# One kernel, two ways of holding P: some thirds of the attention weights kept as one float32 copy

## The chip, the cores and the metric

The kernel runs on one core of a Trainium2 chip. The core has a matrix engine (TensorE; PE in the profile, with PEld for its weight loads), a vector engine (VectorE, DVE), an activation engine (ScalarE, ACT), a general engine (GpSimd, POOL) and a queue that starts transfers (SyncE, SP). Each works through its own instructions in order, and they wait for each other by semaphores. On-chip memory has 128 partitions; TensorE writes its results to a small second memory, PSUM. The metric is the time of one execution on the device, in microseconds (us).

## The reference

Pooled attention over 4 batches and 8 heads, then two feed-forward layers. In float32:

```
q, k, v : (4, 8, 1152, 64)
q_pool = q.reshape(B, H, S // 2, 2, D).mean(axis=3)          # 576 queries
scores = matmul(q_pool, k^T) / sqrt(D)                       # 576 x 1152
attn   = exp(scores - max);  attn = attn / (sum + 1e-9)
x      = matmul(attn, v)                                     # -> (2304, 512)
h  = x @ w_in ;  g  = maximum(0.01 * h, h) ;         y   = g  @ w_out    # 512 -> 2048 -> 512
h2 = y @ w_in2;  g2 = where(h2 > 0, h2, exp(min(h2,0)) - 1); out = g2 @ w_out2
```

The weights of both layers arrive as 64-bit floats and are turned into float32 on the chip.

## The kernel before

**How float32 products are made.** TensorE is used with the type `float32r`, in which one pass goes over float32 numbers at reduced precision. To keep precision, each operand is split into two parts, hi (the value rounded to that type) and lo (the value less hi). `psplit` (line 256) makes them: ACT or DVE copies to hi, DVE or POOL subtracts. A product then takes two or three matmuls.

**Attention.** Heads are worked in pairs, 16 pairs in all (4 per batch), by `attn_pair` (line 550). A pair has nine tiles of 128 query rows: four for each head and one that holds the last 64 rows of both. For a tile, `scores` (line 434) computes three thirds of 384 keys in PSUM (line 452), DVE takes the maxima (lines 457, 459), ACT takes the exponentials with their sums into the tile `p` (line 463). `transpose_p` (line 469) then turns each third round: three transposes on TensorE (line 475), and out of PSUM twice, first by ACT as hi (line 261 of `psplit`) and then, once that is done, by DVE as lo (line 267). They land in a tile `pt`, one for each third, of which four buffers exist (`PTB`). `pv` (line 485) multiplies: for each third, three chunks of 128 keys, with hi and lo, so six matmuls (line 496) of 256 or 320 query columns. Its stationary operand `vn` holds v's hi part in 64 columns and its lo part in the other 64, so the two halves of the result are added afterwards (lines 507 and 509). A pair has four such calls, over 256, 320, 320 and 256 columns. `normalise` (line 511) divides by the sums.

**Feed-forward.** `mlp` runs each layer of each batch in 16 steps `f`: up (line 629) and down (line 667) matmuls of 288 columns, with the activation between (lines 640 to 650) and the sums of the output (line 680). `load_w` brings the weights, and `convert` (line 273; DVE at lines 293, 296 and 305, ACT at 299 and 301, POOL at 303) turns 64-bit into 32-bit. This happens once per layer; later batches load the kept result.

**What sets the order.** All work is entered into `Program` as pieces with an engine, a cost in nanoseconds, a rank and dependencies. Before the program is built a list schedule with these costs fixes the order of the pieces on every engine: whenever an engine is free, the ready piece with the lowest rank goes next. A pair takes nine ranks; the feed-forward of batch b begins when that batch's four pairs are done and shares the time of the next batch's pairs. For the last batch both layers come after the last pair.

The costs of the pieces concerned are written at the calls: three transposes 3 x 107 ns, P V for a third `6 * max(107, 0.42 * n)`.

Of the kernel before, what the change touches and what calls it, by code (L numbers as in the profile page):

```python
# [9 lines left out]
F32 = mybir.dt.float32  # L10
F32R = mybir.dt.float32r
U32 = mybir.dt.uint32
ACTF = mybir.ActivationFunctionType
# [141 lines left out]
def kernel(  # L155
# [20 lines left out]
    V, A, G, PE = nc.vector, nc.scalar, nc.gpsimd, nc.tensor  # L176
# [5 lines left out]
    NP = H // 2  # L182
# [8 lines left out]
    PTB = 4  # L191
# [17 lines left out]
    WLEAD = 1.5  # L209
    SBUFS = 3  # L210
    RAWB = 3
    EARLY = {'s': 'sss', 't': 'tthh'}
    T1B = 3
    HBUFS = 2
# [7 lines left out]
    ORDER = (0, 1, 2)  # L222
# [3 lines left out]
    PVLAG = 0.5  # L226
# [8 lines left out]
    def f32(ap):  # L235
        return ap.bitcast(F32)
# [4 lines left out]
    prog = Program()  # L241

    def sb(tag, shape, dt=F32, bufs=1):
        return prog.buf(tag, bufs, lambda: sp.tile(shape, dt, tag=tag, name=tag, bufs=bufs))

    def bank(tag, shape, dt=F32, bufs=1):
        return prog.buf(tag, bufs, lambda: ps.tile(shape, dt, tag=tag, name=tag, bufs=bufs))

    def act(n, accum=False, sbuf=False):
        return 50 + 0.833 * n + (190 if accum else 0) + (43 if sbuf else 0)  # L250

    def dve(n, fast=False):
        return 66 + (0.52 if fast else 1.05) * n
# [4 lines left out]
    def psplit(rank, h, l, hi, lo, src, n, w, r, w_l=None, fast=True, psum=False):  # L258

        if h == "ACT":  # L260
            prog.add("ACT", act(n, sbuf=not psum), rank, lambda: A.activation(out=hi(), in_=src(), func=ACTF.Copy), w=[w], r=r)  # L261
        else:
            prog.add("DVE", dve(n, fast), rank, lambda: V.tensor_copy(out=hi(), in_=src()), w=[w], r=r)
        eng = V if l == "DVE" else G
        prog.add(
            l, dve(n) if l == "DVE" else pool(n), rank,
            lambda: eng.tensor_tensor(out=lo(), in0=src(), in1=f32(hi()), op=ALU.subtract),  # L267
            w=[w_l or (w[0], "l")], r=[w] + r)
# [69 lines left out]
    for j in range(2):  # L338
        t = sp.tile([128, 2, 128], F32R, name=f"rem{j}")
# [6 lines left out]
    def load(rank, key, tag, shape, pieces, bufs):  # L346
        t = sb(tag, shape, F32, bufs)
        for i, (to, src) in enumerate(pieces):
            prog.add("SP", 60, rank, lambda to=to, src=src: nc.sync.dma_start(out=to(t), in_=src), w=[(t, i)])
        raw[key] = t  # L350

    def load_kq(rank, b, hp, j):
        h = 2 * hp + j
        load(rank, (b, hp, j, "k"), "raw", [128, KC, D],
             [(lambda t: t.ap, k[b, h].rearrange("(p c) d -> p c d", c=KC))], RAWB)
        load(rank, (b, hp, j, "q"), "raw", [128, KC, D],
             [(lambda t: t[:, 0:2 * QT, :], q[b, h, 0:256 * QT].rearrange("(p r) d -> p r d", r=2 * QT))], RAWB)

    def load_v(rank, b, hp, j):
        load(rank, (b, hp, j, "v"), "raw", [128, KC, D],  # L360
             [(lambda t: t.ap, v[b, 2 * hp + j].rearrange("(p c) d -> p c d", c=KC))], RAWB)

    def load_rem(rank, b, hp):
        load(rank, (b, hp, "x"), "qrem", [128, 2, D],
             [(lambda t, j=j: t[64 * j:64 * j + 64],
               q[b, 2 * hp + j, 256 * QT:S].rearrange("(p r) d -> p r d", r=2)) for j in range(2)], 2)
# [37 lines left out]
    def prep_q(rank, b, hp, j):  # L404
        qn = q_split(rank, raw[b, hp, j, "q"], QT, "q")
        qT = sb("qT", [128, 2, QT, 128], F32R, KTB)
        for a in range(2):
            t = tr_r(rank, (qn, a), lambda i, a=a: qn[:, a, i, :], QT)
            prog.add("ACT", act(512), rank, lambda t=t, a=a: A.activation(
                out=qT[:, a], in_=f32(t.ap), func=ACTF.Copy), w=[qT], r=[t])  # L410
        prep[b, hp, j, "q"] = qT
# [20 lines left out]
    def pbank(use, dt=F32, shape=(128, 4, 128)):  # L432
        tags = (EARLY if first_window[0] else {}).get(use, use)
        n = turns[use] = turns.get(use, -1) + 1
        tag = tags[n % len(tags)]
        return bank(tag, list(shape), dt, BANKS[tag])
# [29 lines left out]
                w=[(p, c), (total, (idx, c))], r=[banks[c], (m, 3)])  # L466
        return p

    def transpose_p(rank, p, dests):
        for c in ORDER:  # L470
            t = pbank("t")

            def tr(t=t, c=c):
                for i in range(3):
                    PE.transpose(  # L475
                        out=t[:, i, :], in_=p[:, (3 * c + i) * 128:(3 * c + i + 1) * 128],
                        identity=ident)

            prog.add("PE", 3 * 107, rank, tr, w=[t], r=[(p, c)])
            for pt, c0, s0, n in dests:  # L480
                hi = lambda a=0, pt=pt, c=c, c0=c0, n=n: pt[c][:, a, :, c0:c0 + n]
                psplit(rank, "ACT", "DVE", hi, lambda hi=hi: hi(1), lambda t=t, s0=s0, n=n: t[:, 0:3, s0:s0 + n],
                       3 * n, (pt[c], ("h", c0)), [t], (pt[c], ("l", c0)), fast=False, psum=True)

    def new_pt(n):
        pt = {c: sb("pt", [128, 2, 3, n], F32R, PTB) for c in ORDER}
        return pt

    def pv(rank, b, hp, j, pt, col0, n):
        o = pbank("o", F32, (128, 512))  # L490
        vn = prep[b, hp, j, "v"]

        def mm(th):
            for c in range(3 * th, 3 * th + 3):
                for a in range(2):
                    PE.matmul(  # L496
                        out=o[:, 0:n], lhsT=vn[:, c, :], rhs=pt[th][:, a, c % 3, :],
                        start=(c == 3 * ORDER[0] and a == 0), stop=(c == 3 * ORDER[2] + 2 and a == 1))

        for th in ORDER:  # L500
            prog.add("PE", 6 * max(107, 0.42 * n), rank + PVLAG, lambda th=th: mm(th), w=[o], r=[vn, pt[th]])
        if (b, hp) not in xu:
            xu[b, hp] = sb("xu", [128, NQ], F32, XFB)
        x = xu[b, hp]
        hi, lo = slice(64 * j, 64 * j + 64), slice(64 - 64 * j, 128 - 64 * j)
        tm = sb("tm", [128, 5 * 64])
        prog.add("ACT", act(n), rank + PVLAG, lambda: A.activation(
            out=tm[hi, 0:n], in_=o[lo, 0:n], func=ACTF.Copy), w=[tm], r=[o])
        prog.add("DVE", dve(n), rank + PVLAG, lambda: V.tensor_tensor(
            out=x[hi, col0:col0 + n], in0=o[hi, 0:n], in1=tm[hi, 0:n], op=ALU.add),  # L510
            w=[(x, (j, col0))], r=[o, tm])
# [37 lines left out]

    def attn_pair(at, b, hp, nxt):  # L550
        pts = {}
        n1 = 128 + 128 + RQ
        sums[b, hp] = sb("sum", [128, n9, 3], F32, 2)

        def tile_(at, j, t, g, c0, new=None):
            qT = prep[b, hp, j, "q"]
            p = scores(at, b, hp, [(j, qT, lambda a: qT[:, a, t, :])], 2 * t + j)
            if new:
                pts[j, g] = new_pt(new)
            transpose_p(at, p, [(pts[j, g], c0, 0, 128)])  # L560

        if nxt:
            load_kq(at, *nxt, 0)
            load_rem(at, *nxt)
            load_v(at + 2, *nxt, 0)
            load_kq(at + 3, *nxt, 1)
            load_v(at + 4, *nxt, 1)
        tile_(at, 0, 0, 0, 0, 256)
        prep_k(at + PREP, b, hp, 1)
        prep_q(at + PREP, b, hp, 1)  # L570
        tile_(at + 1, 0, 1, 0, 128)
        prep_rem(at + PREP, b, hp)
        pv(at + 1, b, hp, 0, pts[0, 0], 0, 256)
        prep_v(at + 1, b, hp, 1)
        tile_(at + 2, 0, 2, 1, 0, n1)
        tile_(at + 3, 0, 3, 1, 128)
        p = scores(at + 4, b, hp, [
            (j, rem_t[j], lambda a, j=j: rem_t[j][:, a, :]) for j in range(2)], 2 * QT)
        pts[1, 1] = new_pt(n1)
        transpose_p(at + 4, p, [(pts[0, 1], 256, 0, 64), (pts[1, 1], 256, 64, 64)])  # L580
        pv(at + 4, b, hp, 0, pts[0, 1], 256, n1)
        tile_(at + 5, 1, 2, 1, 0)
        tile_(at + 6, 1, 3, 1, 128)
        if nxt:
            prep_k(at + 5, *nxt, 0)
            prep_q(at + 5.5, *nxt, 0)
            prep_v(at + 6, *nxt, 0)
        pv(at + 6, b, hp, 1, pts[1, 1], 256, n1)
        tile_(at + 7, 1, 0, 0, 0, 256)
        tile_(at + 8, 1, 1, 0, 128)  # L590
        pv(at + 8, b, hp, 1, pts[1, 0], 0, 256)
        normalise(at + 8 + PVLAG + 0.2, b, hp)


# [136 lines left out]
    for b, layer, at, wide in PLAN:  # L731
        tags = [(u, size[u]) for u in ("h" * HBUFS + ("t" * TB + "s" * SBUFS if wide else ""))]
        w = ((moe_w_in, moe_w_out), (moe2_w_in, moe2_w_out))[layer]
# [35 lines left out]
```

## Time and profile before

| | |
|---|---|
| median of 3 runs | 1545.18 us (1543.68 to 1550.88) |
| the profiled execution, as a run | 1545.34 us |
| its span in the trace | 1543.5 us |
| PE busy | 1414.5 us (92%) |
| PEld busy | 1365.2 us (88%) |
| DVE busy | 1011.4 us (66%) |
| ACT busy | 1065.9 us (69%) |
| POOL busy | 830.3 us (54%) |
| granted TensorE clock | 0.99 of 2.4 GHz on average |

Shares are averages over stages that differ: in the first 16 of 40 equal slices DVE is at 8 or 9 tenths in all but the very first; after them it falls to 6 and less while PE goes to 9 in nearly all. The end of a matmul in the trace is modelled, and matmuls overlap, so what one costs is read from the distance between starts (a run of n of them, divided), and "PE busy" holds some overlap of one group's tail with the wait behind it.

### The profile page before, as it was taken

The page shows a single profiled execution, that of the slowest core. Times are in us where ns is not written, and L with a number is a line of the kernel's source. Part 1 is how long each engine was busy: PE and PEld are TensorE (multiplying, and loading weights), DVE is VectorE, ACT ScalarE, POOL GpSimd, SP SyncE. Part 2 cuts the span into 40 slices and gives each one's busy share as a digit, 9 for nine tenths or more (in the row PEclk, how much of TensorE's full clock was granted, in tenths as well). Part 3 has the DMA queues.
Part 4 walks back from the last instruction along what each step waited for, and adds up shares of the span by engine and source line. Part 5 has one row for each costly group of instructions (what it writes and reads, how often), then busy time and mean ns, then how long its engine had stood idle before and what let it go on. Part 6 is the DMA issues. An engine that isn't in the chain of part 4 may idle for free.

```text
span 1543.5 us, 28953 instructions
## 1 busy us (share of the span) xinstructions
PE 1414.5 (92%) x10288; PEld 1365.2 (88%) x10288; DVE 1011.4 (66%) x2273; ACT 1065.9 (69%) x2901; POOL 830.3 (54%) x840
## 2 busy tenths in 40 slices
PE   5878889888888898999999999999999999899997
PEld 4777788888878887999999999899999998899897
DVE  6999889899998998556565556645665554124222
ACT  6989878776678787676668776676667763443553
POOL 5443255765766667254555556254554445466662
PEclk9999999999999999999999999999999999999999
DMA  4332123343334443222222222222221121322221
GB/s 138 99 115 87 40 75 123 121 130 125 126 118 144 130 143 120 74 71 73 67 69 86 79 78 63 74 76 66 71 67 59 55 56 56 93 76 82 69 82 39
DMA packets 82642, 135.59 MB, mean 88 GB/s; under 512 B 8512, under 2 KB 26944, under 8 KB 82496
## 3 DMA queue, kind: packets, MB, share of 16 engines
q1 hardware_dynamic: 82496, 133.73, 28.0%
q8 instruction: 81, 1.33, 0.4%
q14 instruction: 65, 0.53, 0.1%
HBM read 112.20 MB, written 21.50 MB: 87 GB/s over the span
## 4 chain that ended last, share of the span: by engine, by line
PE 64%; DVE 21%; ACT 6%; issue 3%; DMA 3%; POOL 2%; SPq 0%; ACTq 0%; POOLq 0%; DVEq 0%
PE h L667 17%; PE h L629 16%; PE s L452 8%; PE o L496 7%; PE t L475 5%; DVE m L457 3%; PE s L629 3%; DVE ct L293 3%; DVE wr L305 3%; DVE ct L296 3%; DVE pt L267 2%; PE s L667 2%; PE t L373 2%; PE t L629 2%; PE t L667 2%
## 5 line engine op out<-in xcount | busy, mean ns | idle before, releaser
L667 PE MATMUL h<-g,wo 128*128 128x288 f32 x2544 | 437.1, 302 | 17.5 <-DVE t L650 7.9
L629 PE MATMUL h<-xs,wi 128*128 128x288 f32 x2520 | 429.2, 305 | 22.9 <-DVE t L650 14.2
L629 PEld LDWEIGHTS h<-xs,wi 128*128 128x128 f32 x2520 | 362.5, 190 | 32.5 <-DVE t L650 20.0
L667 PEld LDWEIGHTS h<-g,wo 128*128 128x128 f32 x2544 | 367.1, 188 | 23.8 <-DVE t L650 9.6
L457 DVE TENSOR_REDUCE m<-s 128x1 f32<-128x384 f32 x432 | 232.2, 550 | 74.4 <-PE s L452 71.6
L261 ACT ACTIVATE pt<-t 128x384 fp32r<-128x384 f32 (+1 forms) x416 | 184.0, 457 | 115.2 <-PE t L475 108.3
L463 ACT ACTIVATE p<-s,m 128x384 f32<-128x384 f32 x432 | 249.5, 588 | 18.3 <-DVE m L459 18.0
L267 DVE TENSOR_TENSOR pt<-t,pt 128x384 fp32r<-128x384 f32 (+1 forms) x416 | 206.8, 509 | 73.3 <-ACT pt L261 71.7
L267 POOL TENSOR_TENSOR g<-t,g 128x288 fp32r<-128x288 f32 x256 | 211.1, 831 | 79.9 <-ACT g L261 75.5
L267 POOL TENSOR_TENSOR wo<-wr,wo 128x512 fp32r<-128x512 f32 x128 | 166.4, 1304 | 137.5 <-ACT wo L261 134.3
L452 PE MATMUL s<-kT,qT 128*128 128x384 f32 x768 | 197.0, 354 | 25.4 <-ACT p L463 24.5
L267 POOL TENSOR_TENSOR wi<-wr,wi 128x512 fp32r<-128x512 f32 x128 | 167.6, 1309 | 91.9 <-ACT wi L261 79.3
L496 PE MATMUL o<-pt,vn 128*128 128x256 f32 (+1 forms) x1152 | 192.5, 303 | 5.5 <-DVE pt L267 3.6
L475 PE MATMUL t<-ident,p 128*128 128x128 f32 x1116 | 181.6, 277 | 12.4 <-DVE pt L267 11.7
L496 PEld LDWEIGHTS o<-pt,vn 128*128 128x128 f32 x1152 | 165.5, 190 | 10.6 <-DVE pt L267 10.2
L475 PEld LDWEIGHTS t<-ident,p 128*128 128x128 f32 x1116 | 139.4, 142 | 22.1 <-DVE pt L267 12.3
L452 PEld LDWEIGHTS s<-kT,qT 128*128 128x128 f32 x768 | 125.5, 192 | 32.2 <-ACT p L463 31.0
L303 POOL TENSOR_TENSOR ct<-ct,cr 128x256 uint32<-128x256 uint32 x128 | 98.8, 774 | 96.7 <-DVE ct L296 29.8
L261 ACT ACTIVATE g<-t 128x288 fp32r<-128x288 f32 x256 | 112.2, 445 | 49.0 <-DVE t L650 28.4
L267 POOL TENSOR_TENSOR vn<-raw,vn 128x576 fp32r<-128x576 f32 x32 | 46.4, 1449 | 174.4 <-ACT vn L261 174.4
L261 ACT ACTIVATE wo<-wr 128x512 fp32r<-128x512 f32 x128 | 80.6, 630 | 78.9 <-PE h L667 47.5
L680 DVE TENSOR_TENSOR acc<-h,acc 128x288 f32<-128x288 f32 x158 | 71.1, 452 | 67.2 <-PE h L667 66.1
(106 smaller groups left out, 2080.0 us busy)
## 6 DMA issues: line engine op xcount, KB each, us to landing
wr<-w SPq DMA_DIRECT2D x192, 256.0 KB, 2.6
cr<-in_moe_w_in_dram SPq DMA_DIRECT2D x64, 256.0 KB, 2.7
cr<-in_moe_w_out_dram SPq DMA_DIRECT2D x64, 256.0 KB, 2.7
w<-wr SPq DMA_DIRECT2D x64, 256.0 KB, 2.4
raw<-in_k_dram SPq DMA_DIRECT2D x32, 288.0 KB, 3.0
raw<-in_v_dram SPq DMA_DIRECT2D x32, 288.0 KB, 3.1
raw<-in_q_dram SPq DMA_DIRECT2D x32, 256.0 KB, 2.9
out_dram<-cr SPq DMA_DIRECT2D x16, 256.0 KB, 2.1
```

The lines of the kernel that those rows point to most:

```text
L261: prog.add("ACT", act(n, sbuf=not psum), rank, lambda: A.activation(out=hi(), in_=src(), func=ACTF.Copy), w=[w], r=r)
L267: lambda: eng.tensor_tensor(out=lo(), in0=src(), in1=f32(hi()), op=ALU.subtract),
L293: prog.add("DVE", dve(CW, True), rank, lambda r=r, t=t: V.tensor_scalar(out=t.ap, in0=r[:, :, 1], scalar1=3, scalar2=0x3FFFFFF8, op0=ALU.l ...
L303: prog.add("POOL", pool(CW), rank, lambda t=t, r=r: G.tensor_tensor(out=t.ap, in0=t.ap, in1=r[:, :, 0], op=ALU.add), w=[t], r=[t, (r, 0)])
L452: PE.matmul(out=st[:, 0:384], lhsT=qa(a), rhs=kT[:, 384 * c:384 * c + 384], start=(i == 0), stop=(i == len(seq) - 1))
L457: prog.add("DVE", dve(384), rank - LR, lambda st=st, c=c: V.tensor_reduce(out=m[:, c:c + 1], in_=st[:, 0:384], axis=AX.X, op=ALU.max), w=[ ...
L463: prog.add("ACT", act(384, True), rank - LE, lambda c=c: A.activation(out=p[:, 384 * c:384 * c + 384], in_=banks[c][:, 0:384], func=ACTF.E ...
L475: PE.transpose(out=t[:, i, :], in_=p[:, (3 * c + i) * 128:(3 * c + i + 1) * 128], identity=ident)
L496: PE.matmul(out=o[:, 0:n], lhsT=vn[:, c, :], rhs=pt[th][:, a, c % 3, :], start=(c == 3 * ORDER[0] and a == 0), stop=(c == 3 * ORDER[2] + 2 ...
L629: PE.matmul(out=h[:, 0:HB], lhsT=wi[:, a, c, :], rhs=xs[c][:, e, cols], start=(c == 0 and a == 0 and e == 0), stop=(c == DC - 1 and a == 1))
L667: PE.matmul(out=y[:, 0:HB], lhsT=w[f][1][:, a, d * 128:(d + 1) * 128], rhs=g[f][:, e, cols], start=(f % FC == 0 and a == 0 and e == 0), st ...
L680: prog.add("DVE", dve(HB), rank - HURRY, lambda y=y, a_=a_, cols=cols: V.tensor_tensor(out=a_[:, cols], in0=y[:, 0:HB], in1=a_[:, cols], o ...
```

## The change

In the first batch (pairs 0 to 3) two of the three key thirds of P, and in pairs 4 to 9 one, are no longer split. The transposed third is copied out of PSUM once, as float32, by DVE or by ACT (`WHOLE` says which), and `pv` multiplies it by v's two stacked parts read as float32, in three matmuls in place of six. The list schedule gets a new cost for these pieces, 5.25 ns per column for a third as float32, and 2.76 for one in two parts in place of `6 * max(107, 0.42 * n)`. The other thirds, and pairs 10 to 15, are computed as before.

```diff
+    WHOLE = ({0: "DVE", 1: "ACT"}, {0: "ACT"})
+    WPAIRS = 10
...
-    def transpose_p(rank, p, dests):
+    def transpose_p(rank, p, dests, whole):
         for c in ORDER:
             t = pbank("t")
+            how = whole.get(c)
...
             prog.add("PE", 3 * 107, rank, tr, w=[t], r=[(p, c)])
             for pt, c0, s0, n in dests:
+                if how:
+                    o, i_ = (lambda pt=pt, c=c, c0=c0, n=n: pt[c][:, :, c0:c0 + n],
+                             lambda t=t, s0=s0, n=n: t[:, 0:3, s0:s0 + n])
+                    if how == "ACT":
+                        prog.add("ACT", act(3 * n), rank, lambda o=o, i_=i_: A.activation(
+                            out=o(), in_=i_(), func=ACTF.Copy), w=[(pt[c], ("h", c0))], r=[t])
+                    else:
+                        prog.add("DVE", dve(3 * n), rank, lambda o=o, i_=i_: V.tensor_copy(
+                            out=o(), in_=i_()), w=[(pt[c], ("h", c0))], r=[t])
+                    continue
                 hi = lambda a=0, pt=pt, c=c, c0=c0, n=n: pt[c][:, a, :, c0:c0 + n]
                 psplit(rank, "ACT", "DVE", hi, lambda hi=hi: hi(1), lambda t=t, s0=s0, n=n: t[:, 0:3, s0:s0 + n],
                        3 * n, (pt[c], ("h", c0)), [t], (pt[c], ("l", c0)), fast=False, psum=True)
 
-    def new_pt(n):
-        pt = {c: sb("pt", [128, 2, 3, n], F32R, PTB) for c in ORDER}
+    def new_pt(n, whole):
+        pt = {c: sb("pt", [128, 3, n], F32, PTB) if c in whole else sb("pt", [128, 2, 3, n], F32R, PTB) for c in ORDER}
         return pt
...
             for c in range(3 * th, 3 * th + 3):
-                for a in range(2):
+                for a in range(1 if th in whole else 2):
                     PE.matmul(
-                        out=o[:, 0:n], lhsT=vn[:, c, :], rhs=pt[th][:, a, c % 3, :],
+                        out=o[:, 0:n], lhsT=f32(vn[:, c, :]) if th in whole else vn[:, c, :],
+                        rhs=pt[th][:, c % 3, :] if th in whole else pt[th][:, a, c % 3, :],
                         start=(c == 3 * ORDER[0] and a == 0), stop=(c == 3 * ORDER[2] + 2 and a == 1))
 
         for th in ORDER:
-            prog.add("PE", 6 * max(107, 0.42 * n), rank + PVLAG, lambda th=th: mm(th), w=[o], r=[vn, pt[th]])
+            prog.add("PE", (5.25 if th in whole else 2.76) * n, rank + PVLAG, lambda th=th: mm(th), w=[o], r=[vn, pt[th]])
...
     def attn_pair(at, b, hp, nxt):
         pts = {}
+        whole = WHOLE[0] if b == 0 else WHOLE[1] if NP * b + hp < WPAIRS else {}
...
```

Two places show what this makes of the order. On DVE, in pair 0, the two tiles after the sum over the first 320 columns (`m` maxima, `pt` the transposed thirds, `ct` and `wr` the weight conversion, `t` and `h` PSUM buffers). Before:

```order
L509 TENSOR_TENSOR xu<-o,tm 64x320
L459 TENSOR_REDUCE m<-m 128x1
L267 TENSOR_TENSOR pt<-h,pt 128x3x128 x2
L267 TENSOR_TENSOR pt<-t,pt 128x3x128
L296 SCALAR_TENSOR_TENSOR ct<-cr,ct 128x256
L457 TENSOR_REDUCE m<-s 128x1 x2
L267 TENSOR_TENSOR pt<-t,pt 128x3x128
L457 TENSOR_REDUCE m<-s 128x1
L267 TENSOR_TENSOR pt<-h,pt 128x3x128
```

The same place in the change:

```order
L461 TENSOR_REDUCE m<-m 128x1
L491 COPY pt<-h 128x3x128
L524 TENSOR_TENSOR xu<-o,tm 64x320
L307 SCALAR_TENSOR_TENSOR wr<-cm,ct 128x256 x2
L269 TENSOR_TENSOR pt<-t,pt 128x3x128
L295 TENSOR_SCALAR ct<-cr 128x256 x2
L459 TENSOR_REDUCE m<-s 128x1
L491 COPY pt<-t 128x3x128
L459 TENSOR_REDUCE m<-s 128x1 x2
```

Of three subtractions for a tile one stays, one is a copy and one is gone; conversion moves into the place. Over the whole program DVE issues 372 instructions at the subtraction's line in place of 512 at its line before (32 of either number split the feed-forward's inputs), and 40 copies at line 491. In the first batch the conversions stand earlier: 22 of 128 blocks are begun before the second pair is normalised, 17 before; by the fourth pair it is 22 in both.

On TensorE, in pair 0, the first P V call over 320 columns (`o` its result, `s` the scores of the tiles that follow). Before:

```order
L475 MATMUL t_527<-ident_58,p_492 128x128 x3
L496 MATMUL o_536<-pt_411,vn_173 128x320 x6
L496 MATMUL o_536<-pt_418,vn_173 128x320 x6
L452 MATMUL s_567<-kT_235,qT_304 128x384 x2
L496 MATMUL o_536<-pt_424,vn_173 128x320 x6
L452 MATMUL s_588<-kT_235,qT_304 128x384 x2
L452 MATMUL s_595<-kT_235,qT_304 128x384 x2
```

In the change:

```order
L478 MATMUL t_521<-ident_58,p_484 128x128 x3
L510 MATMUL o_527<-pt_412,vn_173 128x320 x3
L510 MATMUL o_527<-pt_424,vn_173 128x320 x3
L454 MATMUL s_558<-kT_244,qT_304 128x384 x2
L454 MATMUL s_564<-kT_244,qT_304 128x384 x2
L454 MATMUL s_570<-kT_244,qT_304 128x384 x2
L510 MATMUL o_527<-pt_433,vn_173 128x320 x6
```

The first two thirds are three matmuls each, the last one stays at six, and the next tile's scores now stand together between them.

## Rows read from the trace of the kernel before

**Rows 1.** Busy time of each engine by stretch: length, PE, PEld, DVE, ACT, POOL, clock
```profile
18.00:156.00 138.00, 111.94 (x747) 101.77 (x747) 125.10 (x310) 124.14 (x359) 60.08 (x62) 0.96 0.31 100
156.00:199.00 43.00, 35.65 (x256) 32.55 (x256) 36.00 (x87) 36.42 (x105) 12.12 (x13) 1.00 0.14 41
199.00:267.00 68.00, 62.42 (x442) 58.81 (x442) 59.13 (x141) 56.26 (x162) 36.24 (x39) 0.97 0.33 108
267.00:590.00 323.00, 280.96 (x1983) 262.30 (x1982) 303.31 (x637) 245.05 (x687) 213.06 (x224) 0.99 0.40 130
590.00:670.00 80.00, 71.62 (x511) 69.36 (x510) 50.29 (x112) 54.89 (x147) 44.39 (x44) 0.96 0.29 91
670.00:755.00 85.00, 85.00 (x646) 84.60 (x644) 48.32 (x112) 58.17 (x158) 43.29 (x42) 1.00 0.25 75
755.00:1274.00 519.00, 511.60 (x3865) 506.77 (x3864) 306.79 (x704) 367.33 (x995) 261.66 (x253) 1.00 0.23 67
1274.00:1544.00 270.00, 249.97 (x1830) 245.05 (x1828) 73.21 (x161) 116.13 (x278) 147.97 (x147) 0.98 0.24 71
```

**Rows 2.** Waits in 18 to 199 us: who for whom, total us, times, longest
```profile
PE s L452 <- ACT p L463: 28.3, 17, 4.6
DVE m L457 <- PE s L452: 10.4, 15, 2.6
ACT pt L261 <- PE t L475: 7.1, 14, 1.6
```

**Rows 3.** Waits in 267 to 590 us
```profile
PE h L629 <- DVE t L650: 11.0, 12, 1.7
ACT g L261 <- DVE t L642: 13.2, 14, 2.6
ACT g L261 <- DVE t L650: 11.1, 12, 1.8
```

**Rows 4.** Groups by line and shape in 199 to 590 us: the conversion's DVE instructions
```profile
L305 DVE SCALAR_TENSOR_TENSOR wr<-cm,ct 128x256 f32<-128x256 f32 x106 | 73.8, 701 | 1.5 <-POOL ct L303 1.4
L296 DVE SCALAR_TENSOR_TENSOR ct<-cr,ct 128x256 uint32<-128x256 uint32 x105 | 68.6, 656 | 0.8
L293 DVE TENSOR_SCALAR ct<-cr 128x256 uint32<-128x256 uint32 x106 | 56.6, 537 | 3.6 <-DMA cr<-in_moe_w_in_dram 1.8 <-DMA cr<-in_moe_w_out_dram 1.6
```

**Rows 5.** Groups by line and shape, whole span: busy us, mean ns, idle before
```profile
L267 DVE TENSOR_TENSOR pt<-t,pt 128x384 fp32r<-128x384 f32 x328 | 177.5, 551 | 56.7 <-ACT pt L261 55.5
L267 DVE TENSOR_TENSOR pt<-t,pt 128x192 fp32r<-128x192 f32 x88 | 29.3, 351 | 16.6 <-ACT pt L261 16.2
L261 ACT ACTIVATE pt<-t 128x384 fp32r<-128x384 f32 x328 | 156.4, 490 | 92.5 <-PE t L475 90.5 <-PE s L452 1.0
L261 ACT ACTIVATE pt<-t 128x192 fp32r<-128x192 f32 x88 | 27.6, 333 | 22.7 <-PE t L475 17.8 <-PE o L496 3.3 <-PE s L452 1.0
L457 DVE TENSOR_REDUCE m<-s 128x1 f32<-128x384 f32 x432 | 232.2, 550 | 74.4 <-PE s L452 71.6
L525 DVE COPY rb<-r 128x512 f32<-128x512 f32 x16 | 10.5, 654 | 0.3
```

**Rows 6.** Chain that ended last, 590 to 760 us: P V over 320, then 256 columns
```profile
634.80 0.89 PE o L496 x6
...
677.98 0.70 PE o L496 x6
```

**Rows 7.** Timeline of PE: float32 transposes (L475) and float32r ones (L373), start, length
```profile
26.38 0.49 PE L475 MATMUL h<-ident,p 128*128 128x128 f32 x3
...
34.77 0.82 PE L475 MATMUL h<-ident,p 128*128 128x128 f32 x6
...
23.81 0.24 PE L373 MATMUL t<-identr,qn 128*128 128x128 f32 x1
...
657.74 0.37 PE L373 MATMUL t<-identr,kn 128*128 128x128 f32 x3
```

More of the change, by code (lines that the diff above doesn't have):

```diff
@@ L483, in transpose_p, with pv @@
                        3 * n, (pt[c], ("h", c0)), [t], (pt[c], ("l", c0)), fast=False, psum=True)
-    def new_pt(n):
-        pt = {c: sb("pt", [128, 2, 3, n], F32R, PTB) for c in ORDER}
+    def new_pt(n, whole):
+        pt = {c: sb("pt", [128, 3, n], F32, PTB) if c in whole else sb("pt", [128, 2, 3, n], F32R, PTB) for c in ORDER}
         return pt
-    def pv(rank, b, hp, j, pt, col0, n):
+    def pv(rank, b, hp, j, pt, col0, n, whole):
         o = pbank("o", F32, (128, 512))
@@ L558, in tile_ @@
             if new:
-                pts[j, g] = new_pt(new)
-            transpose_p(at, p, [(pts[j, g], c0, 0, 128)])
+                pts[j, g] = new_pt(new, whole)
+            transpose_p(at, p, [(pts[j, g], c0, 0, 128)], whole)
         if nxt:
@@ L572, in attn_pair @@
         prep_rem(at + PREP, b, hp)
-        pv(at + 1, b, hp, 0, pts[0, 0], 0, 256)
+        pv(at + 1, b, hp, 0, pts[0, 0], 0, 256, whole)
         prep_v(at + 1, b, hp, 1)
@@ L578, in attn_pair @@
             (j, rem_t[j], lambda a, j=j: rem_t[j][:, a, :]) for j in range(2)], 2 * QT)
-        pts[1, 1] = new_pt(n1)
-        transpose_p(at + 4, p, [(pts[0, 1], 256, 0, 64), (pts[1, 1], 256, 64, 64)])
-        pv(at + 4, b, hp, 0, pts[0, 1], 256, n1)
+        pts[1, 1] = new_pt(n1, whole)
+        transpose_p(at + 4, p, [(pts[0, 1], 256, 0, 64), (pts[1, 1], 256, 64, 64)], whole)
+        pv(at + 4, b, hp, 0, pts[0, 1], 256, n1, whole)
         tile_(at + 5, 1, 2, 1, 0)
@@ L587, in attn_pair @@
             prep_v(at + 6, *nxt, 0)
-        pv(at + 6, b, hp, 1, pts[1, 1], 256, n1)
+        pv(at + 6, b, hp, 1, pts[1, 1], 256, n1, whole)
         tile_(at + 7, 1, 0, 0, 0, 256)
         tile_(at + 8, 1, 1, 0, 128)
-        pv(at + 8, b, hp, 1, pts[1, 0], 0, 256)
+        pv(at + 8, b, hp, 1, pts[1, 0], 0, 256, whole)
         normalise(at + 8 + PVLAG + 0.2, b, hp)
```

## The prediction

> **What bounds the kernel now.** I read the busy time by stretch first, cut at the ends of pairs, because the shares of the page mix stages. The reader is to see three different kernels in [rows 1]. From 18 to 199 us (pairs 0 to 3, no feed-forward beside them) DVE is busy 125.1 + 36.0 = 161.1 of 181 us (89%), ACT 160.6 (89%), PE 147.6 (82%): two engines nearly full, the third not far behind. From 199 to 590 us (pairs 4 to 7, the first batch's feed-forward beside them) DVE has 59.1 + 303.3 = 362.4 of 391 us (93%), and 94% after the first 68 us, while PE has 88% and ACT 77%. From 590 us on PE is the bound: 85.0 of 85.0 us in pair 9, 98.6% from 755 to 1274.
>
> Then the waits, for what PE lacks while it isn't full. In the first batch it waits for ACT's exponentials, which must leave a PSUM buffer before new scores go in: 28.3 us in 17 waits, up to 4.6 us [rows 2]. The same list has DVE waiting 10.4 us for scores and ACT 7.1 us for transposes, so this is a loop through three engines and not one engine alone. From 267 us on the waits end at DVE: PE for the activation's result (11.0 us), ACT for the same kind of result (13.2 and 11.1 us) [rows 3]. DVE's load there is the weight conversion: 73.8 + 68.6 + 56.6 = 199 us in 391 [rows 4], which ends at 590 us, and DVE's bound with it.
>
> **What goes from DVE and ACT.** A pair has for each third eight transposed blocks of 384 elements per partition and two of 192 (the ninth tile goes to two destinations). At 551 and 351 ns a block [rows 5] a third's subtractions are 8 x 0.551 + 2 x 0.351 = 5.11 us of DVE; at 490 and 333 ns its hi copies are 4.59 us of ACT. A third kept whole by ACT loses the 5.11 us of DVE; one kept whole by DVE loses ACT's 4.59 us and exchanges a DVE subtraction for a DVE copy. No copy out of PSUM by DVE is in the trace. The nearest row, a maximum over the same 384 PSUM elements, takes 550 ns; a copy of 512 takes 654, in proportion 490 for 384 [rows 5]. I take 550, so no change; with 490 it would be another 32 x 0.06 = 2 us off, and as much on if it were as much dearer. In sum: pairs 0 to 3 lose 20.4 us of DVE and 18.3 us of ACT; pairs 4 to 7 lose 20.4 us of DVE; pairs 8 and 9 lose 10.2 us of DVE, where nobody waits for it. The chain of a whole third is also one step shorter: its product waits for one copy, not for a copy and then a subtraction.
>
> **What PE gains.** Now a third has six matmuls in 0.89 us over 320 columns and in 0.70 over 256 [rows 6], so 148 and 117 ns, 0.46 ns a column; a third of one pair has 256 + 320 + 320 + 256 = 1152 columns, 6 x 0.46 x 1152 = 3.18 us. In its place come three float32 matmuls over the same columns, of which no product is in the trace. Three bounds from rows. If they ran at the same rate, 1.59 us: 1.6 us saved. The float32 transposes show that the type costs more: three more of them take 0.82 - 0.49 = 0.33 us, 110 ns each, against (0.37 - 0.24) / 2 = 65 ns for float32r [rows 7], so about 1.7 times. There only one operand holds data. If a float32 product takes twice the time of a float32r one, a third costs 3.18 us as now, no change; if each of its two operands doubles the time, four times, it costs 6.36 us, 3.18 more. The list schedule of the change charges 5.25 ns a column, 6.05 us. Its charges for what the trace does show fit the rows (2.76 x 320 = 883 ns against 0.89 us, 3 x 107 against 3 x 110), and it lies by the upper bound, so I take it: 6.05 - 3.18 = 2.87 us more for a third of a pair. With eight thirds in pairs 0 to 3 that is 23.0 us, with one in each of pairs 4 to 7 11.5, in pairs 8 and 9 5.7; 40 us in all, and from -22 to +45 by the bounds.
>
> The Trainium skill ("FP8 and Floating Point Precision", TensorE Precision Notes) says that a true float32 product makes four passes through the array. That speaks for the upper bound, and no run here shows it so far. As an estimate from it, 12 x 1152 columns at 2.4 GHz are 5.76 us, 2.6 more than now, and the whole sum would come out about 2 us lower.
>
> **What of it is on the path.** *Pairs 0 to 3.* DVE's 161.1 us become 140.7, ACT's 160.6 become 142.3, PE's 147.6 become 170.6 of 181 us. The share that must then be packed tightest is PE's. Could it be? Its busy time includes the tails of groups in front of waits. By distances between starts a pair holds 60 score matmuls of 384 columns at 0.46 ns a column (10.6 us), 81 transposes of P at 110 ns (8.9), P V (9.5), and some 41 transposes of k, q and the sums at 65 to 110 (about 3): 32 us of the 45 that a pair takes, 38 afterwards. So PE needs 4 x 38 = 152 us at least, and DVE and ACT 141. What PE waited for, ACT's exponentials, comes sooner with ACT 11% less loaded. With none of three engines above 91% I put the stretch at 168 us, 13 less: 90.5% for PE's 152. If DVE stayed the bound at its 89%, it would be 20.4 / 0.89 = 23 less; if PE could not be packed better than its waits allow now, 0. Pair 3 argues for the lower half: without conversion it still took 43 us with no engine above 85% [rows 1].
>
> *Pairs 4 to 7.* DVE gives back 20.4 us of 362.4. At the same 93%, that is 22 us. But PE's 343.4 us grow by 11.5 to 355, of 391: at 22 less it would have 96%. And in pair 4 PE is already at 92% and DVE only at 87%, so I count nothing there. I take 13 less, 85% of the 15.3 us that DVE loses in pairs 5 to 7, which leaves PE at 94%. Bounds 0 and 22.
>
> *Pairs 8 and 9.* PE's 5.7 us lie on the path: PE has 156.6 of 165 us, and what it lacks is in pair 8. I count 5.
>
> *The rest.* Pairs 10 to 15 and the last layers are as before; that they come in another order I put at zero, plus or minus 3. By the order the same work stands between the ends of pairs from pair 8 on. Queued behind a float32 product on PE are the next tile's scores or the feed-forward's matmuls: a third of 320 columns takes 1.68 us for 0.88, so DVE's maxima come up to 0.8 us later for each whole third. The buffers of P are held as much longer, and the copies of the next query group wait for them, at ACT and DVE; this is why I don't take the full gain in either stretch.
>
> Sum: -13 - 13 + 5 = -21 us, against the profiled execution's own 1545.3 (span 1543.5), which the median of 1545.2 hardly differs from: 1524 us.
>
> **The rivals.**
>
> *PE takes the bound in pairs 0 to 7.* The in-order queue puts the float32 product in front of the scores, PE's waits of 28.3 us for exponentials [rows 2] stay, since they come from the loop and not from ACT's load, and what DVE saves ends as idle time. For it: pair 3's 43 us with three engines at 83 to 85%. Against it: ACT and DVE are near 90% together before, and both are relieved. Halfway, pairs 0 to 3 gain 3, pairs 4 to 7 gain 4, pairs 8 and 9 lose 5: 1543. Chance 0.13.
>
> *The same, past that point: slower.* The added 23 us of PE come on top of its waits in pairs 0 to 3. It decides when PE's busy time there plus the waits that stay exceeds the present 181 us: 170.6 + 10 or more, so when more than a third of the 28.3 us stays. If all stay it is 199, 18 more; pairs 4 to 7 gain nothing, pairs 8 and 9 lose 5: 1568. If two thirds stay, 1559. Chance 0.10.
>
> *DVE decides alone, and PE's additions hide in both stretches.* -23 - 22 + 5 = -40: 1505. For it: 94% of DVE from 267 to 590 us and the waits that end at DVE [rows 3]. Against: PE at 96% with three other engines feeding it. Chance 0.12.
>
> *The float32 product costs no more than the two that it replaces*, as the transposes' 1.7 times would have it. Nothing is added on PE: about -18 - 18 = -36, 1509. Against it: two operands instead of one. Chance 0.05.
>
> By the rule of the four passes none of these changes its place; it only makes the last one unlikely.
>
> **How the numbers follow.** The forecast has 0.60; its own range is 1512 to 1536 (7 to 10 us on either side for the packing in the two stretches, 3 for the order). A measurement of this kernel tells about 0.5% from no change, 7.7 us: faster is under 1537.5, slower over 1552.9. Faster: 0.60 + 0.12 + 0.05 + 0.01 of the first rival = 0.78; same 0.12; slower 0.10. The range for 8 in 10 goes from 1506, which leaves out half of the two quicker rivals, to 1546, which takes in the first rival and leaves out the slower one.
>
> **What would show it.** Right: P V matmuls of 320 columns 560 ns apart in whole thirds; the end of pair 3 near 186 instead of 199 us; the conversion's end near 564 instead of 590; pairs 8 and 9 about 5 us longer in sum, and the same time as before from there to the end. In the first batch PE busy above 90% and its wait for exponentials halved. Wrong: pair 3 ends at 195 or later with PE waiting as long as before; or the span from 590 to the end grows by more than 5 us; or the matmuls lie 300 ns apart.

## The result: 0.9% slower, and the profile after

The change took 1560.5 us (median of 5 runs, 1555.0 to 1560.8) where the kernel before took 1549.2 beside it: 1.0093 times, interval 1.0073 to 1.0113, by the ratio on record; the two medians alone, 11.3 us apart, give 1.0073. Run again later it was 1.0080 (1.0059 to 1.0100). The forecast was 1524 and faster. The profiled execution has 1560.8 us and a span of 1559.0, 15.5 more than the profiled one before. That one has 1545.3 us, low among the five beside the change, but like the medians of 1544.4 to 1546.4 that its kernel has in the longer sets of runs behind. These 15.5 us are what is placed here.

Busy time by stretch in the change (length, PE, PEld, DVE, ACT, POOL, clock), cut at its own pair ends, to lay beside [rows 1]:

```profile
18.00:156.00 138.00, 118.70 (x713) 102.90 (x714) 113.31 (x270) 111.27 (x321) 59.66 (x61) 0.98 0.31 98
156.00:205.00 49.00, 44.49 (x283) 38.46 (x283) 34.87 (x85) 35.74 (x103) 13.00 (x14) 1.00 0.15 42
205.00:271.00 66.00, 61.34 (x426) 56.86 (x427) 57.30 (x130) 53.71 (x155) 34.40 (x37) 1.00 0.34 108
271.00:590.00 319.00, 278.01 (x1939) 260.35 (x1938) 291.86 (x606) 246.15 (x683) 212.55 (x222) 0.99 0.41 131
590.00:673.00 83.00, 78.61 (x561) 75.41 (x560) 49.34 (x107) 58.21 (x154) 45.59 (x45) 0.98 0.29 87
673.00:763.00 90.00, 90.00 (x664) 88.36 (x663) 44.18 (x102) 58.99 (x159) 44.19 (x44) 1.00 0.25 74
763.00:1286.00 523.00, 515.25 (x3860) 508.80 (x3858) 304.36 (x702) 367.52 (x995) 261.42 (x253) 0.99 0.23 67
1286.00:1559.00 273.00, 253.56 (x1834) 248.62 (x1833) 73.19 (x161) 115.99 (x278) 147.79 (x147) 0.97 0.25 70
```

In pairs 0 to 3 DVE fell to 148.2 us (161.1 before) and ACT to 147.0 (160.6), less far than the 140.7 and 142.3 worked out. PE rose from 147.6 to 163.2 us, and the stretch grew: pair 3's sums are reduced at 201.9 us, 196.6 before. Such a mark, the reduction of a pair's sums, is read here for the end of a pair. It scatters by up to 3 us between executions (the change has 204.9 in a second profile; four kernels whose first four pairs are those of before have 196.6 to 199.1), and it doesn't stand behind the same work everywhere: up to it PE has issued 1009 matmuls in the kernel before and 997 in the change. Pairs 4 to 7 then take 379.0 us from that mark to the same one of pair 7 (384.5). This is less of a gain than it looks: PE issued 426 + 1939 = 2365 matmuls from 205 to 590 us where it had issued 442 + 1983 = 2425 from 199 to 590, so 60 of them, 8 us at the 133 ns from start to start of those of 288 columns, were handed on. From pair 7's mark to pair 9's it is 175.6 us for 168.2. Two rows show what lay there, before and in the change:

```profile
581.10:749.30 168.20, 158.94 (x1169) 155.84 (x1168) 102.70 (x230) 119.01 (x321) 91.51 (x91) 0.98 0.29 87
```
```profile
580.90:756.50 175.60, 171.21 (x1240) 166.13 (x1239) 97.82 (x221) 121.24 (x325) 91.07 (x91) 0.99 0.28 83
```

71 matmul entries more, and 48 of the entries there, those of 24 float32 products, are dearer. The other 8.3 us come after pair 9, where the change has the same instructions as before.

What the float32 product costs, from the timeline of PE in pair 9 (six entries each: float32, then the split third, at 256 and at 320 columns):

```profile
682.16 1.46 PE L510 MATMUL o<-pt,vn 128*128 128x256 f32 x6
...
684.97 0.87 PE L510 MATMUL o<-pt,vn 128*128 128x256 f32 x6
...
728.71 1.78 PE L510 MATMUL o<-pt,vn 128*128 128x320 f32 x6
...
732.00 1.05 PE L510 MATMUL o<-pt,vn 128*128 128x320 f32 x6
```

Each float32 matmul appears as two entries, so the count at this line is 1152 as before. A third of a pair has two calls of each width: 2 x (1.46 - 0.87) + 2 x (1.78 - 1.05) = 2.64 us dearer, some 37 us over 14 thirds. The span grew by 15.5, so waits, clock and order together gave back about 21.

Waits from 18 to 205 us in the change, to lay beside [rows 2]; the last row here had 4.3 us in 5 waits before:

```profile
PE s L454 <- ACT p L465: 18.8, 14, 4.6
DVE m L459 <- PE s L454: 13.7, 16, 2.8
ACT tm L522 <- PE o L510: 13.6, 9, 2.3
```

PE's wait for exponentials shrank by a third, not by the half or more that the forecast needed. In its place ACT and DVE now wait for PE: for the P V result and for scores.

From 271 to 590 us the waits that end at DVE are shorter than in [rows 3], with one that ends at a transfer of the conversion's input, which had less than 4 us before, beside them:

```profile
ACT cr L301 <- DMA cr<-in_moe_w_in_dram: 15.6, 12, 3.7
...
ACT g L263 <- DVE t L666: 9.1, 12, 1.4
PE h L645 <- DVE t L666: 7.6, 7, 2.1
...
ACT g L263 <- DVE t L658: 6.5, 8, 1.4
```

### The profile page after: what moved, and what is told of

It reads as the page before. It is cut to its first block, busy times and chain, and to the rows that moved or that the text cites. A ratio compares the mean times of both kernels' runs of the same rounds, so it can differ in the third digit from the quotient of the medians.

```text
span 1559.0 us, 28852 instructions
## 1 busy us (share of the span) xinstructions
PE 1445.3 (93%) x10288; PEld 1383.8 (89%) x10288; DVE 977.7 (63%) x2173; ACT 1055.1 (68%) x2861; POOL 830.1 (53%) x840
## 3 DMA queue, kind: packets, MB, share of 16 engines
q1 hardware_dynamic: 82496, 133.73, 28.3%
## 4 chain that ended last, share of the span: by engine, by line
PE 59%; DVE 14%; ACT 7%; DMA 5%; issue 4%; POOL 2%; ACTq 0%; SPq 0%; DVEq 0%; POOLq 0%
PE h L683 16%; PE h L645 15%; PE o L510 7%; PE s L454 7%; PE t L478 5%; PE s L645 3%; DVE wr L307 2%; PE s L683 2%; DMA cr<-in_moe_w_in_dram 2%; DVE m L459 2%; DVE ct L295 2%; DVE ct L298 2%; PE t L683 2%; PE t L645 2%; PE t L375 2%
## 5 line engine op out<-in xcount | busy, mean ns | idle before, releaser
L683 PE MATMUL h<-g,wo 128*128 128x288 f32 x2544 | 446.2, 304 | 15.3 <-DVE t L666 10.8
L645 PE MATMUL h<-xs,wi 128*128 128x288 f32 x2520 | 424.4, 305 | 21.7 <-DVE t L666 9.7
L683 PEld LDWEIGHTS h<-g,wo 128*128 128x128 f32 x2544 | 371.6, 190 | 20.5 <-DVE t L666 13.4
L510 PE MATMUL o<-pt,vn 128*128 128x256 f32 (+1 forms) x1152 | 222.2, 330 | 2.0 <-DVE pt L491 2.0
L269 DVE TENSOR_TENSOR pt<-t,pt 128x384 fp32r<-128x384 f32 (+1 forms) x312 | 155.4, 508 | 80.1 <-ACT pt L263 78.7
L263 ACT ACTIVATE pt<-t 128x384 fp32r<-128x384 f32 (+1 forms) x312 | 138.1, 455 | 95.6 <-PE t L478 90.5
L510 PEld LDWEIGHTS o<-pt,vn 128*128 128x128 f32 x1152 | 177.5, 189 | 16.1 <-DVE pt L491 3.5
```

Of the source, the lines that this page charges most:

```text
L510: PE.matmul(out=o[:, 0:n], lhsT=f32(vn[:, c, :]) if th in whole else vn[:, c, :], rhs=pt[th][:, c % 3, :] if th in whole else pt[th][:, a, ...
L645: PE.matmul(out=h[:, 0:HB], lhsT=wi[:, a, c, :], rhs=xs[c][:, e, cols], start=(c == 0 and a == 0 and e == 0), stop=(c == DC - 1 and a == 1))
L683: PE.matmul(out=y[:, 0:HB], lhsT=w[f][1][:, a, d * 128:(d + 1) * 128], rhs=g[f][:, e, cols], start=(f % FC == 0 and a == 0 and e == 0), st ...
```

## Experiments

Theories: *PE theory*: the product's time on TensorE is not hidden, and what DVE and ACT save in the first batch is mostly idle time, since a pair there is a loop through three engines. *Order theory*: the list schedule's new charges put all the work in another order, and that costs the time. *Forecast's theory*: DVE bounds pairs 0 to 7. *Loop theory*, which the PE theory takes in: a pair without conversion beside it takes as long as the round of scores, maxima, exponentials and transposes between the engines, whatever the load of one of them. Each kernel's ratio is to the kernel before on the same chip, with its interval.

**The charge alone.** The kernel before, with one number changed:

```diff
-            prog.add("PE", 6 * max(107, 0.42 * n), ...
+            prog.add("PE", 2.76 * n, ...
```


> The kernel before, with nothing but the list schedule's charge for a P V third put from 6*max(107, 0.42n) to 2.76n, as the change has it for its split thirds; no third is kept whole. PE theory: no work is added, within 3 us of before. Order theory: 6 us slower or more.


Measured 1550.1 us, 1.0033 (1.0021 to 1.0046). That is between the two ranges expected. Not one instruction differs, and 5 us are lost. As much is lost by the end of pair 3 (201.9 us), but PE has issued 1026 matmuls by then, 17 more than before, so some 2 of those 5 us are work that stands earlier. The step "I put the order at zero, plus or minus 3" failed. The old charge is 2.52 ns a column; I also tried 2.9:

> The kernel before with the P V charge at 2.9n, no third whole: same instructions as before, another order. With 2.76n it was 5 us slower. Scatter theory: between 0 and 8 us slower than before, and not the same as at 2.76n. Theory that a higher charge is worse for the list throughout: 5 us slower or more.


1549.1 us, 1.0022 (1.0008 to 1.0035): slower than at 2.52, not slower than at 2.76 (the two intervals overlap).

**The change with the old charge** for the thirds that stay split:

```diff
-            prog.add("PE", (5.25 if th in whole else 2.76) * n, ...
+            prog.add("PE", 5.25 * n if th in whole else 6 * max(107, 0.42 * n), ...
```


> The whole change, with the list schedule's old charge 6*max(107, 0.42n) for the thirds that stay split (the new 5.25n for whole ones). Order theory (the new charge for split thirds costs about 5 us by moving conversion into pair 1, as with the charge alone): 4 to 8 us faster than the change, 8 to 10 us slower than before. PE theory alone: within 3 us of the change.


1548.1 us, 1.0017 (1.0003 to 1.0030). The same instructions as the change, which had 1.0093: about 12 us were its order, more than either theory expected. It ends pair 3 at 202.0, as late as the change; the difference lies behind. The change again, and at other charges (the text below calls 2.9 between 2.76 and the old charge; it lies beyond it):

> The change itself once more, beside the following kernels on one chip. Both theories: 1.0073 to 1.0113 times the time of before, as measured. If it comes within 0.3% of the kernel with the old charge for split thirds (1.0017), the charge's 12 us were a difference of chips and runs.

> The change with the list schedule's charges at 5.1n for a whole third and 2.9n for a split one in place of 5.25n and 2.76n; the same instructions in another order. If the order's cost lies in the value 2.76 being wrong for the list, 2.9 lies between it and the old charge (107 a matmul is 2.5n at 256 columns, 0.42n a matmul is 2.52n at 320): no use is expected from it, the time stays at the change's, within 3 us. If any other order of the same work scatters, it lands anywhere from 5 us above before to 15 above.


1557.1 us, 1.0080 (1.0059 to 1.0100), and 1565.5 us, 1.0138 (1.0116 to 1.0159). The second is beyond all that was expected. So one and the same work took from 1548.1 to 1565.5 us in three orders, by the ratios up to 19 us apart. One place of it can be read: behind pair 11 in the change ACT waits for a transfer of weights (4.49 us in the chain of waits), the copy that PE needs stands behind it in ACT's queue, and PE, full up to 996.5 us, is busy for 1.9 of 4.2 us from 997.0 on. Then its granted clock is 0.50, the level of 1.2 GHz, from 1001.2 to 1008.0 us. In the row of before for the same place, the second one, it stays at 1.00, as it does in the kernel with the old charge from 980 to 1003 us:

```profile
1000.00:1008.00 8.00, 7.32 (x33) 6.41 (x32) 3.16 (x6) 4.48 (x13) 0.74 (x1) 0.57 0.68 217
```
```profile
985.00:1000.00 15.00, 12.14 (x90) 11.07 (x90) 7.50 (x18) 10.97 (x29) 5.20 (x5) 1.00 0.39 119
```

**Relief without the product's price.** Copies as in the change, but the whole third is rounded to float32r and multiplied six times, the same part twice, its lo part left out:

```diff
-        pt = {c: sb("pt", [128, 3, n], F32, PTB) if c in whole ...
+        pt = {c: sb("pt", [128, 3, n], F32R, PTB) if c in whole ...
...
-                for a in range(1 if th in whole else 2):
+                for a in range(2):
-                        out=o[:, 0:n], lhsT=f32(vn[:, c, :]) if th in whole else vn[:, c, :],
+                        out=o[:, 0:n], lhsT=vn[:, c, :],
```


> All copies and subtractions as in the change (one copy of a whole third, in pairs 0 to 9), but the third is rounded to float32r and multiplied by six float32r matmuls (the same operand twice, so the result is another): DVE and ACT are relieved as in the change and TensorE has the work of before. PE theory: it is the product that cost the gain; pair 3 ends 8 to 18 us earlier than before, pairs 4 to 7 take 10 to 18 us less, pairs 8 and 9 the same: 18 to 36 us faster than before. Loop theory (in the first batch no engine's load sets the time, only the latency round the loop): pair 3 ends within 3 us of before, the gain is that of pairs 4 to 7 alone, 7 to 15 us.


With the new charge (2.76 for all) 1535.1 us, 0.9940 (0.9926 to 0.9953). That is in the range of the loop theory, with pair 3 at 198.4 us, and little more than half of the 18 us that the PE theory expected at least. With the old charge:

> The cheap product (whole thirds rounded to float32r and multiplied by six float32r matmuls) with the list's old charge for all P V pieces: relief of DVE and ACT alone, in nearly the old order. If relief and charge simply add, 15 us under the kernel before (0.990), since it was 10 under it with the new charge, which alone cost 5. If the charge only matters where TensorE is full, 10 us (0.994) as with the new charge.


1531.0 us, 0.9913 (0.9893 to 0.9933): 13.4 us, near the sum of 15, and that is all that relieving DVE and ACT was worth with nothing to pay on PE. The forecast had put it at about 36 (its fourth rival).

**The product's price without relief.** Split everywhere, the chosen thirds multiplied twice, by twelve float32r matmuls, 14 x 3.18 = 45 us of PE:

```diff
-            how = whole.get(c)
+            how = None
...
-                for a in range(1 if th in whole else 2):
+                for i, a in enumerate((0, 1, 0, 1) if th in whole else (0, 1)):
```


> P is split in every third as before, so DVE and ACT keep all their work, and the thirds that the change keeps whole are multiplied twice, with twelve float32r matmuls in place of six (the result is another): TensorE gets about 44 us of added work, the change 38. PE theory: hardly any of it hides, since relieved DVE and ACT are what took some 20 us of waits away in the change; 30 to 45 us slower than before. Forecast's theory (PE has room for it in pairs 0 to 7 beside a busy DVE): 5 to 15 us slower.

> The dear product alone (P split everywhere, the chosen thirds multiplied by twelve float32r matmuls), old charge for the other thirds: 45 us of TensorE's work without relief. Adding: 33 us over the kernel before (38 less 5; 1.021). If the charge costs more where TensorE has more to do, 26 us or less (1.017).


1584.2 us, 1.0244 (1.0219 to 1.0268), with the new charge and 1589.7, 1.0296 (1.0273 to 1.0319), with the old: 38 and 46 us for 45. The first is in the PE theory's range; the second lies above the 33 and the 26 expected. Beside a busy DVE none of it hides with the old charge. The pair without conversion shows it; 177.7 to 228.5 us is pair 3 of the kernel with the old charge:

```profile
177.70:228.50 50.80, 43.15 (x304) 40.27 (x304) 34.99 (x87) 36.63 (x105) 11.99 (x12) 0.97 0.13 36
```

50.8 us for 42.8, with six more matmuls in each of eight thirds, 6.4 us. Charge and product do not add: the new charge costs 5 us alone, 4 with relief, 8 less than nothing with the product, 10 to 12 with both. Nor do relief and product: by themselves -13 and +46 us (in proportion some +38 for the 37 us of the float32 product), together +2.6.

**How much relief the first batch can use.** The cheap product with the third third whole as well, in pairs 0 to 3:

```diff
-    WHOLE = ({0: "DVE", 1: "ACT"}, {0: "ACT"})
+    WHOLE = ({0: "DVE", 1: "ACT", 2: "ACT"}, {0: "ACT"})
```


> As the kernel with the cheap product (whole thirds rounded to float32r, six matmuls), with all three thirds of P whole in pairs 0 to 3, the third one copied by ACT: DVE loses another 20 us there, TensorE and ACT nothing. Loop theory (round trip between the engines, not their load, sets a pair without conversion beside it): pair 3 ends within 3 us of the kernel with the cheap product (198 us). Load theory (DVE's share is what is left): pair 3 ends at 185 to 192 us.


1528.7 us, 0.9881 (0.9854 to 0.9907); pair 3 ends at 196.6 us. Pair 3 with two thirds cheap, with all three, and in the change:

```profile
157.50:198.50 41.00, 34.55 (x259) 32.40 (x258) 29.94 (x79) 33.05 (x95) 12.08 (x13) 1.00 0.16 44
```
```profile
156.00:196.50 40.50, 34.22 (x256) 32.20 (x256) 26.03 (x67) 32.74 (x95) 11.93 (x13) 1.00 0.15 45
```
```profile
160.00:205.00 45.00, 40.82 (x255) 35.06 (x256) 31.52 (x78) 32.73 (x95) 12.02 (x12) 1.00 0.14 40
```

The reader is to see a floor: DVE goes from 36.0 us [rows 1] over 29.9 to 26.0, 64% of the pair, and the pair from 43 to 41 (40.7 with the old charge) to 40.5. No engine is above 85% in either. In the change the pair takes 45 with DVE and ACT at 70 and 73% and PE at 91%: relief took 2 us off it, and the product, 5.3 us of PE's time for two thirds, put 4 on. With all three thirds cheap the waits from 115 to 196 us close the circle:

```profile
DVE m L459 <- PE s L454: 22.6, 23, 1.7
...
PE s L454 <- ACT p L465: 11.6, 10, 1.5
...
ACT pt L488 <- PE t L478: 7.0, 8, 2.0
```

This is what the loop theory expected of a pair without conversion. In the kernel before conversion filled pairs 0 to 2 (8, 7 and 5 blocks) and made DVE look like the bound; in the change it sits in pairs 0 and 1 (10 and 10). Pair 2 had 45.6 us with five blocks and has 45.2 with none.

**Which pairs.** With the tables alone changed (new charge):

```diff
-    WHOLE = ({0: "DVE", 1: "ACT"}, {0: "ACT"})
+    WHOLE = ({0: "DVE", 1: "ACT"}, {})        # pairs 0 to 3
+    WHOLE = ({}, {0: "ACT"}) ; WPAIRS = 8     # pairs 4 to 7
```


> Thirds of P kept whole in pairs 0 to 3 alone (two of three), none afterwards. PE theory (the float32 product's extra time on TensorE, some 23 us there, is not hidden, since the loop of scores, exponentials and transposes already has PE near full): pair 3 ends about 5 us later than before, all later stretches take their old time, so 4 to 7 us slower than before in all. Order theory (the list's new charges move work everywhere, and that costs the time): most of the 15 us of the whole change stays. Forecast's theory (DVE bounds the first batch): 10 us faster.

> One third of P kept whole in pairs 4 to 7 alone. PE theory: there PE has room beside DVE's conversion, so the stretch from pair 4 to pair 7 is 6 to 8 us shorter, with nothing lost before or after it: 5 to 8 us faster than before. Order theory: 0 to 8 us slower.


1549.4 us, 1.0039 (1.0023 to 1.0054), and 1544.6, 0.9996 (0.9983 to 1.0009). The first lies in the PE theory's range, but it is what the charge alone costs, so it says nothing for that theory. The second misses the 5 to 8 us of the PE theory, loses 5 us by the end of pair 3 (201.3), where nothing but the order differs from before, and gets it back. With the old charge:

> One third kept whole in pairs 4 to 7 alone, with the old charge for split thirds. Order theory: pair 3 ends at 197 us as before, and pairs 4 to 7 keep their small gain: 3 to 8 us faster than before. PE theory alone: as with the new charge, within 2 us of before.

> Two whole thirds in pairs 0 to 3 alone, old charge for split thirds. PE theory: the change with the old charge is 3 us over before, pairs 4 to 7 alone are 5 under, so pairs 0 to 3 and 8 to 9 hold 8; 2 to 5 us over before (1.002). If the first batch's 5 us were the charge's, 0 or less.

> One whole third in pairs 8 and 9 alone, old charge. TensorE is the bound there and gets 5.4 us of work, nobody waits for the relieved DVE: 4 to 6 us over before (1.003).


Pairs 4 to 7: 1540.5 us, 0.9966 (0.9952 to 0.9980), with pair 3 at 196.7 as before. Pairs 0 to 3: 1543.0, 0.9995 (0.9980 to 1.0010), not the 2 to 5 us over before that the PE theory expected: pair 3 ends at 199.9, 3.3 us later than before, and the stretches behind it give that back. Pairs 8 and 9: 1551.4, 1.0044 (1.0027 to 1.0061). In us -5.3, -0.8 and +6.8, in sum +0.7, near the +2.6 of all together: under the old charge the parts add. Pairs 4 to 7 alone is the version that beats both kernels. A second third there:

```diff
-    WHOLE = ({}, {0: "ACT"})
+    WHOLE = ({}, {0: "ACT", 1: "ACT"})
```


> Two thirds whole in pairs 4 to 7, both copied by ACT, old charge for split thirds, nothing whole in pairs 0 to 3 and 8 to 15. DVE loses 20 us more than with one third, TensorE gains 11 more. DVE theory of that stretch (its 93% sets the time up to the conversion's end): conversion ends 10 us earlier still, 3 to 10 us faster than with one third. PE theory: PE has 88 to 92% there already, the second third hides half at best: within 4 us of one third, on the slower side.


1546.5 us, 1.0004 (0.9990 to 1.0018), 6 us above one third, where the PE theory expected at most 4. From 199 to 590 us, with one third and with two:

```profile
199.00:590.00 391.00, 352.04 (x2410) 328.89 (x2411) 347.29 (x747) 304.55 (x850) 249.99 (x262) 0.98 0.39 127
```
```profile
199.00:590.00 391.00, 352.97 (x2370) 326.13 (x2369) 331.18 (x699) 300.74 (x841) 248.29 (x260) 0.99 0.40 127
```

PE is at 90% in both, DVE falls from 89% to 85% for nothing, and PE gets 40 fewer matmuls issued: that speaks for PE as the limit there after the first third. It is argued from these shares; no run gives a second third without its product.

## Why the prediction was wrong

*The price of the product* was right: 2.87 us forecast for a third of a pair, 2.64 measured. The Trainium skill ("FP8 and Floating Point Precision", TensorE Precision Notes) says that a true float32 product makes four passes through the array, and the forecast's estimate from it was 2.6 us. The trace agrees: a product took 3.7 times as long as a float32r one (last section). *The copies* were right too: DVE's of 384 columns out of PSUM takes 549 ns, where 550 was taken.

*Pairs 0 to 3, -13: this step failed.* The end of pair 3 came 5.3 us later in the change, and 3.3 later with the old charge and these pairs alone (199.9 against 196.6), where the whole time is that of before (-0.8 us): neither reckoning has the gain. I read 89% on two engines as a bound and took the added PE time as fitting under it. The busy share was that of a loop with conversion poured into its gaps; with relief alone the four pairs gain 4 us (192.7), with 11 matmuls more done by then, and a pair without conversion came no lower than 40.5 us with DVE at 64%. Onto this loop the product's time came: 8.0 us for 6.4 in pair 3 without relief, 4 for 5.3 with it. The row that said so was used as a hedge only: pair 3, without conversion, 43 us with nobody above 85%.

*Pairs 4 to 7, -13: right in sign, too large.* With the old charge -5.3 by itself. Bounds were 0 and 22, and I took 85% of what DVE loses in pairs 5 to 7. PE seems to have had less room than its 88% of busy time said: a second third of relief brought nothing.

*Pairs 8 and 9, +5*: +6.8 (interval 4 to 9), right.

*The order, zero plus or minus 3: this step failed too.* Between the change with the old charge and with the new lie about 12 us, and the new charge entered the working only as a price of the product; for the order I took it for bookkeeping. Without it the change would have been within 0.3% of before, which was the first rival's outcome.

*The slower rival* had the mechanism, the added PE time coming on top of waits that stay, and named two thirds of the waits as 1559. 18.8 of 28.3 us, two thirds, stayed. But its sum put 9 us into pairs 0 to 3 where the change has 5, and nothing into pairs 4 to 7; the agreement with 1560 rests in part on the order's cost, which it did not have.

*The signs.* Of those named for being wrong, the span from 590 us to the end grew, by 15.5 us, and pair 3 ended behind 195, though PE's wait shrank by a third. The matmuls' distance was as forecast, two entries of 270 ns where 560 in all was named. The conversion's last piece starts at 588.7 us (593.3 before), not near 564.

*In sum*, with the old charge and each group of pairs alone: -0.8, -5.3 and +6.8 us where -13, -13 and +5 were forecast, and 10 to 12 us of order where 0 was.

What remains open: why the new charge gives a worse order. By the end of pair 3 it is behind the old charge by 5 us in the kernels without whole thirds there, by 5.7 with the cheap product (198.4 against 192.7), by 4.0 with whole thirds in pairs 0 to 3 alone (203.9 against 199.9), and by nothing in the change itself (201.9, and 204.9 again, against 202.0), with marks that scatter by 3 us. The sizes of 10 to 20 us with whole thirds are measured, not explained. The halved clock behind pair 11 is one part of them: 6.8 us at half the clock are about 3 us lost.

## What to carry to other kernels

A busy share near 90% on two engines need not be a bound where filler work lies in the gaps: look for a stretch without the filler, and take its length, not its shares, as what relief can reach. Do the two halves of a move between engines alone (here -13 and +46 us): they show what each is worth by itself, but they need not add (+2.6 together here), so do both together too, and stretch by stretch, since only pairs 4 to 7 gained. Where a list schedule sets the order, a new cost in it is a change of its own; time it alone.

## What the runs showed of the hardware

A float32 matmul with two float32 operands is recorded as two entries, about 215 ns apart at 256 columns and 270 at 320 (1.46 - 0.87 = 0.59 us over six entries above the 117 ns of float32r, and 0.73 over 148), so 430 and 540 ns for one product: 3.7 times a float32r one. With relief in place it cost less of the total than without: adding it to the kernel with relief took 16 us of 37 (0.9913 to 1.0017, old charge), and adding 45 us of matmuls without relief took 46.
